# Moving the preparation of head pairs, the first loads and the norm steps within the schedule of a routed-attention and SwiGLU kernel

## The chip, the cores and the metric

The kernel runs on one core of a Trainium2 chip. The metric is the time of one execution in device microseconds, lower is better.

## The reference, cut to what matters

```python
# q, k, v: (4, 8, 768, 64); centroids: (8, 16, 64)
q_assign = argmax(q_n @ c_n, axis=-1)            # 16 clusters
k_assign = argmax(k_n @ c_n, axis=-1)
mask = q_assign[..., :, None] == k_assign[..., None, :]
attn = softmax(where(mask, q @ k.T / 8, -1e9))
x = attn @ v                                     # then per token:
xn = x / rms(x) * rms_g                          # (3072, 512)
out = (silu(xn @ w_gate) * (xn @ w_val)) @ w_out # d_ff 1536
```

## The kernel before

The program is one loop over 288 steps, nine per head, in which the instructions of all engines are written in an order set by hand. A pair of heads therefore takes 18 steps, and there are 16 pairs. A step writes a piece of the scores of the current head and their exponential, from step 96 on a piece of the feed-forward network of an earlier batch, one group of PV matmuls of the previous head, and whatever has been put on that step.

```python
def t_group(g):                      # transposes q or k of one head on PE
    ...
    on_dve = (g % 2 == 0 if pi == 0 else g > 1 if pi == 1 else pi < 6 or g % 2)
    if on_dve: nc.vector.tensor_copy(dst, tp)     # out of PSUM
    else:      nc.scalar.copy(dst, tp)
# casts(), casts_v(): POOL.  assign(): PE, scores against the centroids (sp)
# argmax1(): DVE, tr and mx.  argmax2(): DVE, oh, oh, ohT
# place(): DMA of the one-hot rows into the tiles that the scores read
return [t_group(0..3), casts, assign, argmax1, argmax2, place, casts_v]
...
def pv_norm(slot):                   # attention's own division
    nc.vector.reciprocal(inv, acc[:, :, D:D + 1])
    nc.vector.tensor_tensor(x, acc[:, :, 0:D], inv, op=ALU.mult)
...
def ffn_piece(n, kind, ...):         # kind 0: gp, 1: vp, 2: dp
    # PSUM tiles of gp and vp: two buffers in turn
    # DVE frees gp with uu, and vp with gvT; both are put on the list pend
...
for step in range(NT):
    slot, j = divmod(step, NCH)      # NCH = 9
    score_chunk(slot, j)
    ffn_next(...)
    flush(1)                         # writes out pend but for its last entry
    if slot > 0 and 2 <= j < 2 + ST: pv_group(slot - 1, j - 2)   # j = 2..7
    if slot > 0 and j == 2 + ST:     pv_norm(slot - 1)           # j = 8
    extras(step)                     # preparation, norms, loads
```

Up to step 95 the scores go in chunks of three steps through one wide exponential, and all transposes share one PSUM tile. "RMS norm" below is the second normalization (`ir`, `xn`), which comes after attention.

The softmax here doesn't subtract the row's maximum and nothing guards it: scores larger than these inputs give would overflow.

Of the kernel before, what the change touches and what calls it, by code (L numbers as in the profile page):

```python
# [19 lines left out]
def kernel(  # L20
# [12 lines left out]
    nc = tc.nc  # L33
    B, H, S, D = q.shape
# [10 lines left out]
    NCH = ST * S // CH  # L45
# [33 lines left out]
    def load_part(pi, kind):  # L79
        b, hp = divmod(pi, NP)  # L80
        src, nm = ((q, "q_in"), (k, "k_in"), (v, "v_in"))[kind]
        src = src[b, 2 * hp:2 * hp + 2]
        tl = ld.tile([P, 2, ST * D], F32, name=nm, tag=nm)
        nc.sync.dma_start(out=tl, in_=src.rearrange("h (p t) d -> p h (t d)", p=P))
        loads.setdefault(pi, []).append(tl)

    def load_pair(pi):
        for kind in range(3):
            load_part(pi, kind)

    c_in = const.tile([P, D], F32, name="c_in")
    nc.scalar.dma_start(out=c_in, in_=centroids.rearrange("h c d -> (h c) d"))
    for pi, kinds in ((0, (0, 1)), (1, (0, 1)), (0, (2,)), (1, (2,)), (2, (0, 1, 2))):
        for kind in kinds:
            load_part(pi, kind)
    g_b = const.tile([P, DM], F32, name="g_b")
# [25 lines left out]
    def keep_warm(n):  # L122
        w_ps = ps_first.tile([P, CH], F32, name="w_ps", tag="f")
        for _ in range(n):
            nc.tensor.matmul(w_ps, lhsT=zeros[:, 0:P], rhs=zeros, start=True, stop=True)
# [31 lines left out]
    def w_load(i):  # L157
        if i < 8:
            j, kind = divmod(i, 2)
            c = slice(j * DF // 4, (j + 1) * DF // 4)  # L160
            nc.gpsimd.dma_start(out=(wg, wv)[kind][:, :, c],
                                in_=(moe_w_gate, moe_w_val)[kind][:, c].rearrange("(c p) f -> p c f", p=P))
        else:
            j = i - 8
            nc.gpsimd.dma_start(
                out=wo[:, 3 * j:3 * j + 3, :],
                in_=moe_w_out[j * 3 * P:(j + 1) * 3 * P, :].rearrange("(c p) d -> p c d", p=P))
# [4 lines left out]
    def t_tile(name):  # L172
        nt[0] += 1
        pool, tag = ps_t, "t"
        if "wide" not in late:
            pool, tag = ps_first, "f"
        elif "t" in late and nt[0] % 2:
            pool = late["t"]
        return pool.tile([P, HS], F32, name=name, tag=tag)

    def prep_parts(pi):
        st = pi % NSET
        qk32 = [None]
        state = {}

        def t_group(g):
            a, side = divmod(g, 2)
            if g == 0:
                qk32[0] = prep.tile([P, 4, HS], F32, name="qk32", tag="qk32")
            tp = t_tile("tp")  # L190
            src = loads[pi][side]
            for i in range(TH):
                nc.tensor.transpose(tp[:, i * P:(i + 1) * P], src[:, a, i * P:(i + 1) * P], ident_f)  # L193
            dst = qk32[0][:, g, :]
            on_dve = (g % 2 == 0 if pi == 0 else g > 1 if pi == 1 else pi < 6 or g % 2)
            if on_dve:
                nc.vector.tensor_copy(dst, tp)  # L197
            else:
                nc.scalar.copy(dst, tp)  # L199
            state[g] = tp  # L200

        def casts():
            if pi == 0:
                for g in range(4):
                    a, side = divmod(g, 2)
                    for par in range(2):
                        dst = aug[0][a][0:D, side, par * HS:(par + 1) * HS]
                        src = state[g][par * D:(par + 1) * D, :]
                        if g == 3:
                            nc.vector.tensor_copy(dst, src)  # L210
                        else:
                            nc.scalar.copy(dst, src)
                return
            for a in range(2):
                for par in range(2):
                    nc.gpsimd.tensor_copy(aug[st][a][0:D, :, par * HS:(par + 1) * HS],  # L216
                                          qk32[0][par * D:(par + 1) * D, 2 * a:2 * a + 2, :])

        def casts_v():
            v_in = loads[pi][2]  # L220
            nc.gpsimd.tensor_copy(vbf[st][:, :, :, 0:D],  # L221
                                  v_in[:, :, :].rearrange("p a (t d) -> p a t d", d=D))

        def assign():
            h0 = 2 * (pi % NP)
            sp = t_tile("sp")
            for j in range(4):
                side, a = divmod(j, 2)
                nc.tensor.matmul(sp[32 * j:32 * j + 32, :], lhsT=cbd[:, h0 + a, :, :].rearrange("p c r -> p (c r)"),  # L229
                                 rhs=qk32[0][:, 2 * a + side, :], start=True, stop=True,  # L230
                                 tile_position=(0, 32 * j))
            state["sp"] = sp

        def argmax1():
            tr = prep.tile([P, HS], F32, name="tr", tag="tr")
            nc.vector.transpose(tr, state["sp"])  # L236
            mx = small.tile([P, TH * 4, 2], F32, name="mx", tag="mx")
            trv = tr[:, :].rearrange("p (n c r) -> p n r c", c=NC, r=2)
            nc.vector.tensor_reduce(mx, trv, axis=AX, op=ALU.max)
            state["tr"], state["mx"] = trv, mx  # L240

        def argmax2():
            oh = prep.tile([P, HS], BF16, name="oh", tag="oh")
            nc.vector.tensor_tensor(oh[:, :].rearrange("p (n c r) -> p n r c", c=NC, r=2), state["tr"],  # L244
                                    state["mx"].unsqueeze(3).to_broadcast([P, TH * 4, 2, NC]), op=ALU.is_ge)
            nc.vector.tensor_scalar(oh[0:64, :], oh[0:64, :], scalar1=1.0, scalar2=MASK,
                                    op0=ALU.subtract, op1=ALU.mult)
            ohT = prep.tile([P, HS], BF16, name="ohT", tag="ohT")
            nc.vector.transpose(ohT, oh)
            state["ohT"] = ohT  # L250

        def place():
            ohT = state["ohT"]
            for a in range(2):
                for side in range(2):
                    r = 32 * (2 * side + a)
                    eng = nc.sync
                    if pi == 0:
                        eng = nc.gpsimd if side else nc.scalar
                    eng.dma_start(out=aug[st][a][D:KA, side, :].rearrange("c (r n) -> c r n", r=2),  # L260
                                  in_=ohT[r:r + 2 * NC, :])

        return [lambda: t_group(0), lambda: t_group(1), lambda: t_group(2), lambda: t_group(3), casts, assign, argmax1, argmax2, place, casts_v]


# [167 lines left out]
    def at(step, fn):  # L433
        extra.setdefault(step, []).append(fn)

    T0, T1, T2, T3, CAST, SP, ARG1, ARG2, PLACE, CASTV = range(10)
    p0, p1 = prep_parts(0), prep_parts(1)
# [9 lines left out]
    p1[T0]()  # L447
    p0[ARG2]()
    p0[PLACE]()
    for i in (T1, T2, T3, CAST):  # L450
        p1[i]()
    keep_warm(8)
    for i in (SP, ARG1, ARG2, PLACE, CASTV):
        p1[i]()
    first.close()
    late["wide"] = wide.enter_context(tc.tile_pool(name="ps_wide", bufs=2, space=PSUM))
    load_pair(3)
    at(4, lambda: load_pair(4))
    at(30, lambda: nc.sync.dma_start(out=g_b, in_=moe_rms_g.unsqueeze(0).to_broadcast([P, DM])))
    for pi in range(2, B * NP):  # L460
        base = 2 * NCH * (pi - 2) + {2: 4, 3: 1, 6: 6}.get(pi, 0)
        steps = (0, 2, 4, 6, 7, 9, 10, 12, 12, 10) if pi < 7 else (0, 1, 3, 4, 5, 8, 9, 11, 11, 9)
        for fn, step in zip(prep_parts(pi), steps):
            at(base + step, fn)
        if pi < B * NP - 3:
            at({6: 100, 7: 106}.get(pi, base + 12), lambda pi=pi: load_pair(pi + 3))
    for i, step in enumerate((50, 58, 68, 76, 86, 94, 100, 105, 111, 117, 123, 129)):
        at(step, lambda i=i: w_load(i))
    for b in range(B):
        steps = (9, 9, 10, 10, 11, 12, 13, 15, 17, 19, 20, 22, 24, 26)  # L470
        for fn, step in zip(rms_parts(b), steps):
            at(H * NCH * (b + 1) + step, fn)

    def extras(step):
        for fn in extra.get(step, ()):
            fn()
# [1 line left out]
    for step in range(NT):  # L478
        slot, j = divmod(step, NCH)
# [10 lines left out]
            pv_norm(slot - 1)  # L490
        extras(step)

    for j in range(28):
        if j < LAG:
            ffn_next(2 * FC * (B - 1))
        else:
            ffn_next(NU, tail=True)
        flush(1)
        if 2 <= j < 2 + ST:
            pv_group(NS - 1, j - 2)  # L500
        if j == 2 + ST:
            pv_norm(NS - 1)
        extras(NT + j)
# [32 lines left out]
```

## Time and profile before

The kernel before takes 366.14 us (median of four runs, 365.24 to 367.71; the prediction counts from one of them, 366.76). What matters of the profile, whose span is 364.7 us:

| stage | us | what limits it |
|---|---|---|
| to step 95 | 0 to 79 | PE and ACT in turn, many short waits, half clock for 10.24 us |
| steps 96 to 287 | 79 to 285 | PE, nearly without gaps |
| tail of the feed-forward | 285 to 365 | PE |

### The profile page before, as it was taken

What the parts mean: (1) busy time and instruction counts of PE and PEld (TensorE: products, weight loads), DVE (VectorE), ACT (ScalarE), POOL (GpSimd) and SP (SyncE); (2) the same over time, 40 slices, a digit from 0 to 9 for tenths busy, and PEclk for the clock granted to TensorE, in tenths of its full rate; (3) what the DMA queues carried; (4) which work ended last, traced back from release to release, by engine and by line L of the source; (5) the groups of instructions that cost most, each with busy time, mean ns of one, the idle gap of its engine ahead of it and who ended that gap; (6) DMA issues with size and microseconds to landing.
All of it is one profiled execution on the core that took longest, in us unless ns stands there. A gap on an engine that the chain in (4) does not pass through costs nothing.

```text
span 364.7 us, 7453 instructions
## 1 busy us (share of the span) xinstructions
PE 340.2 (93%) x2930; PEld 204.5 (56%) x2930; DVE 222.0 (61%) x443; ACT 228.0 (63%) x395; POOL 85.8 (24%) x119
## 2 busy tenths in 40 slices
PE   7878997688999999999999999999999979999996
PEld 4446665355666665656565665656666635555542
DVE  4766663667666648695665658695544586555540
ACT  3487888656787776867676767767777343232321
POOL 2554551762414041321204041320000011000000
PEclk9999999679999999999999999999999999999999
DMA  7449499289992310735051001431000013100012
GB/s 242 160 136 291 158 217 209 62 112 113 281 221 103 113 58 25 192 75 168 0 164 38 12 31 36 49 78 38 29 2 31 30 51 86 38 31 29 31 58 86
DMA packets 38242, 35.38 MB, mean 97 GB/s; under 512 B 15072, under 2 KB 35008, under 8 KB 38208
## 3 DMA queue, kind: packets, MB, share of 16 engines
q1 hardware_dynamic: 32080, 30.06, 27.8%
q0 software_dynamic: 5888, 4.77, 9.4%
q8 instruction: 23, 0.38, 0.4%
q10 hardware_dynamic: 240, 0.08, 0.1%
q14 instruction: 11, 0.09, 0.1%
HBM read 28.61 MB, written 6.29 MB: 96 GB/s over the span
## 4 chain that ended last, share of the span: by engine, by line
PE 75%; DVE 13%; ACT 5%; DMA 3%; issue 2%; POOL 1%; ACTq 0%; DVEq 0%
PE dp L401 15%; PE vp L372 15%; PE gp L372 15%; PE sc L287 9%; PE acc L301 7%; PE tp L193 6%; PE scw L287 4%; DVE xn L343 3%; PE sp L229 3%; DMA q_in<-in_q_dram 3%; ACT pT L290 2%; DVE gvT L387 1%; ACT jk L326 1%; DVE oh L244 1%; DVE qk L197 1%
## 5 line engine op out<-in xcount | busy, mean ns | idle before, releaser
L290 ACT ACTIVATE pT<-sc 128x512 bf16<-128x512 f32 x192 | 113.3, 597 | 54.7 <-PE sc L287 53.6
L381 DVE SCALAR_TENSOR_TENSOR uu<-th,gp 128x384 f32<-128x384 f32 x96 | 53.0, 553 | 72.9 <-ACT th L377 72.6
L372 PE MATMUL vp<-xnT,wv 128*128 128x384 bf16 x384 | 78.1, 325 | 2.6 <-DVE gvT L387 2.3
L372 PE MATMUL gp<-xnT,wg 128*128 128x384 bf16 x384 | 78.1, 325 | 1.2 <-DVE uu L381 1.0
L401 PE MATMUL dp<-wo,gvT 128*128 128x512 bf16 x288 | 76.0, 378 | 2.9 <-ACT ob L407 1.5
L377 ACT ACTIVATE th<-gp 128x384 f32<-128x384 f32 x96 | 47.1, 491 | 47.9 <-PE gp L372 44.9
L216 POOL CAST aug<-qk 64x768 bf16<-64x768 f32 x60 | 52.1, 868 | 103.8 <-DVE qk L197 100.6
L301 PEld LDWEIGHTS <-pT 128*128 128x128 bf16 x1152 | 58.5, 98 | 29.1 <-issue 3.4
L287 PE MATMUL sc<-aug 80*128 80x512 bf16 (+1 forms) x256 | 72.9, 326 | 0.0
L301 PE MATMUL acc<-vbf,pT 128*128 128x65 bf16 x1152 | 64.3, 195 | 0.2 <-DVE x L311 0.2
L387 DVE TENSOR_TENSOR gvT<-uu,vp 128x384 bf16<-128x384 f32 x96 | 52.6, 548 | 6.5 <-PE vp L372 1.4
L372 PEld LDWEIGHTS <-wg 128*128 128x128 bf16 x384 | 37.2, 97 | 30.2 <-issue 2.3
L290 ACT ACTIVATE pT<-scw 128x1536 bf16<-128x1536 f32 x32 | 45.0, 1452 | 14.4 <-PE scw L287 14.2
L372 PEld LDWEIGHTS <-wv 128*128 128x128 bf16 x384 | 37.0, 97 | 22.3 <-issue 4.2
L401 PEld LDWEIGHTS <-gvT 128*128 128x128 bf16 x288 | 27.9, 97 | 29.1 <-issue 4.4
L287 PEld LDWEIGHTS <-aug 80*128 80x128 bf16 x384 | 34.0, 98 | 17.7 <-POOL vbf L221 4.4
L197 DVE COPY qk<-tp 128x384 f32<-128x384 f32 x40 | 22.1, 554 | 25.6 <-PE tp L193 25.6
L287 PE MATMUL scw<-aug 80*128 80x512 bf16 (+1 forms) x128 | 27.2, 337 | 1.9 <-DVE tr L236 0.7
L334 POOL TENSOR_SCALAR ir<-ss 128x3 f32<-128x3 f32 x8 | 1.6, 196 | 97.8 <-ACT jk L326 97.8
L343 DVE SCALAR_TENSOR_TENSOR xn<-x,ir,g_b 128x512 bf16<-128x512 bf16 x24 | 20.5, 863 | 5.5 <-POOL ir L335 5.4
L193 PE MATMUL tp<-ident_f,k_in 128*128 128x128 f32 x96 | 17.7, 296 | 5.3 <-ACT qk L199 4.3
L193 PE MATMUL tp<-ident_f,q_in 128*128 128x128 f32 x96 | 17.8, 298 | 3.0 <-DMA q_in<-in_q_dram 2.0
(54 smaller groups left out, 204.2 us busy)
## 6 DMA issues: line engine op xcount, KB each, us to landing
q_in<-in_q_dram SPq DMA_DIRECT2D x16, 384.0 KB, 4.7
k_in<-in_k_dram SPq DMA_DIRECT2D x16, 384.0 KB, 5.1
v_in<-in_v_dram SPq DMA_DIRECT2D x16, 384.0 KB, 5.7
out_dram<-ob SPq DMA_DIRECT2D x24, 256.0 KB, 2.0
wg<-in_moe_w_gate_dram POOLq DMA_DIRECT2D x4, 384.0 KB, 5.4
wv<-in_moe_w_val_dram POOLq DMA_DIRECT2D x4, 384.0 KB, 6.7
wo<-in_moe_w_out_dram POOLq DMA_DIRECT2D x4, 384.0 KB, 7.2
aug<-ohT SPq DMA_DIRECT2D x60, 24.0 KB, 1.9
```

The lines of the kernel that those rows point to most:

```text
L193: nc.tensor.transpose(tp[:, i * P:(i + 1) * P], src[:, a, i * P:(i + 1) * P], ident_f)
L197: nc.vector.tensor_copy(dst, tp)
L216: nc.gpsimd.tensor_copy(aug[st][a][0:D, :, par * HS:(par + 1) * HS], qk32[0][par * D:(par + 1) * D, 2 * a:2 * a + 2, :])
L287: nc.tensor.matmul(sc[:, o:o + n], lhsT=ag[:, 1, kc * P:(kc + 1) * P], rhs=ag[:, 0, qo:qo + n], start=True, stop=True)
L290: nc.scalar.activation(pts[slot][:, j * CH:(j + nch) * CH], sc[:, :nch * CH], ACT.Exp, scale=scale)
L301: nc.tensor.matmul(acc[:, TORD[g], :], lhsT=pts[slot][:, kc * S + g * P:kc * S + (g + 1) * P], rhs=vb[:, a, TORD[kc], :], start=(kc == 0), ...
L343: nc.vector.scalar_tensor_tensor(st["xn"][:, tl, :], x_t[b][:, t, :], st["ir"][:, tl:tl + 1], g_b, op0=ALU.mult, op1=ALU.mult)
L372: nc.tensor.matmul(pt[:, :HS], lhsT=w[:, dc, fc * P:(fc + 1) * P], rhs=xnT[b, m][:, :, dc, :], start=(dc == 0), stop=(dc == DC - 1))
L377: nc.scalar.activation(th, pt[:, :HS], ACT.Tanh, scale=0.5)
L381: nc.vector.scalar_tensor_tensor(uu, th, 1.0, pt[:, :HS], op0=ALU.add, op1=ALU.mult)
L387: nc.vector.tensor_tensor(gvT[half][:, fc, :], uu, pt[:, :HS], op=ALU.mult)
L401: nc.tensor.matmul(dp, lhsT=gvT[hf][:, f, tl * P:(tl + 1) * P], rhs=wo[:, f, :], start=(f == 0), stop=(f == FC - 1))
```

## The change

The intent was to let the first one-hot DMAs pass ahead of the third pair's loads, to start scores before the second pair is assigned, and to prepare each pair earlier, so that preparation and RMS norm do not meet.

```diff
-    for pi, kinds in (..., (1, (2,)), (2, (0, 1, 2))):
+    for pi, kinds in (..., (1, (2,))):
-            on_dve = (... g > 1 if pi == 1 else pi < 6 or g % 2)
+            on_dve = (... g > 0 if pi == 1 else pi < 7 or g % 2)
-                    if pi == 0:
-                        eng = nc.gpsimd if side else nc.scalar
+                    if pi == 0 and side:
+                        eng = nc.gpsimd
...
     p0[PLACE]()
+    load_pair(2)
...
-    for i in (SP, ARG1, ARG2, PLACE, CASTV):
-        p1[i]()
-    load_pair(3)
-    at(4, lambda: load_pair(4))
+    for i, step in ((SP, 0), (ARG1, 0), (ARG2, 1), (PLACE, 1), (CASTV, 1)):
+        at(step, p1[i])
+    at(2, lambda: load_pair(3))
+    at(6, lambda: load_pair(4))
...
-        base = 2 * NCH * (pi - 2) + {2: 4, 3: 1, 6: 6}.get(pi, 0)
-        steps = (0, 2, 4, 6, 7, 9, 10, 12, 12, 10) if pi < 7 else (0, 1, 3, 4, 5, 8, 9, 11, 11, 9)
+        base = 2 * NCH * (pi - 2) + {2: 7, 3: 2}.get(pi, 0)
+        steps = (-3, -1, 1, 3, 4, 6, 7, 8, 8, 10) if pi < 8 else (-3, -2, 0, 1, 2, 5, 6, 7, 7, 10)
...   (the RMS norm, now written ahead of the preparation of the same step)
-        steps = (9, 9, 10, 10, 11, 12, 13, 15, 17, 19, 20, 22, 24, 26)
+        steps = (9, 9, 10, 11, 12, 13, 15, 18, 20, 22, 23, 25, 28, 31)
-    for j in range(28):
+    for j in range(33):
```

The entries of `steps` for preparation are, in order: four transposes, casts, assignment, argmax1, argmax2, place, cast of v.

More of the change, by code (lines that the diff above doesn't have):

```diff
@@ L92 @@
     nc.scalar.dma_start(out=c_in, in_=centroids.rearrange("h c d -> (h c) d"))
-    for pi, kinds in ((0, (0, 1)), (1, (0, 1)), (0, (2,)), (1, (2,)), (2, (0, 1, 2))):
+    for pi, kinds in ((0, (0, 1)), (1, (0, 1)), (0, (2,)), (1, (2,))):
         for kind in kinds:
@@ L194, in t_group @@
             dst = qk32[0][:, g, :]
-            on_dve = (g % 2 == 0 if pi == 0 else g > 1 if pi == 1 else pi < 6 or g % 2)
+            on_dve = (g % 2 == 0 if pi == 0 else g > 0 if pi == 1 else pi < 7 or g % 2)
             if on_dve:
@@ L452 @@
     keep_warm(8)
-    for i in (SP, ARG1, ARG2, PLACE, CASTV):
-        p1[i]()
     first.close()
     late["wide"] = wide.enter_context(tc.tile_pool(name="ps_wide", bufs=2, space=PSUM))
-    load_pair(3)
-    at(4, lambda: load_pair(4))
+    for i, step in ((SP, 0), (ARG1, 0), (ARG2, 1), (PLACE, 1), (CASTV, 1)):
+        at(step, p1[i])
+    at(2, lambda: load_pair(3))
+    at(6, lambda: load_pair(4))
     at(30, lambda: nc.sync.dma_start(out=g_b, in_=moe_rms_g.unsqueeze(0).to_broadcast([P, DM])))
+    for b in range(B):
+        steps = (9, 9, 10, 11, 12, 13, 15, 18, 20, 22, 23, 25, 28, 31)
+        for fn, step in zip(rms_parts(b), steps):
+            at(H * NCH * (b + 1) + step, fn)
     for pi in range(2, B * NP):
-        base = 2 * NCH * (pi - 2) + {2: 4, 3: 1, 6: 6}.get(pi, 0)
-        steps = (0, 2, 4, 6, 7, 9, 10, 12, 12, 10) if pi < 7 else (0, 1, 3, 4, 5, 8, 9, 11, 11, 9)
+        base = 2 * NCH * (pi - 2) + {2: 7, 3: 2}.get(pi, 0)
+        steps = (-3, -1, 1, 3, 4, 6, 7, 8, 8, 10) if pi < 8 else (-3, -2, 0, 1, 2, 5, 6, 7, 7, 10)
         for fn, step in zip(prep_parts(pi), steps):
@@ L468 @@
         at(step, lambda i=i: w_load(i))
-    for b in range(B):
-        steps = (9, 9, 10, 10, 11, 12, 13, 15, 17, 19, 20, 22, 24, 26)
-        for fn, step in zip(rms_parts(b), steps):
-            at(H * NCH * (b + 1) + step, fn)
     def extras(step):
```

## The prediction

> **What bounds the kernel now.** I read the busy shares first, then a table by stage, then the order of time where a stage is not full.
>
> ```profile
> PE 340.2 (93%) x2930; PEld 204.5 (56%) x2930; DVE 222.0 (61%) x443; ACT 228.0 (63%) x395; POOL 85.8 (24%) x119
> ...
> PEclk9999999679999999999999999999999999999999
> ```
>
> ```profile
> 0.00:80.00 80.00, 65.82 (x660) 41.36 (x661) 47.53 (x100) 55.91 (x58) 38.98 (x59) 0.94 0.70 181
> 80.00:100.00 20.00, 18.64 (x185) 11.55 (x183) 14.37 (x29) 14.49 (x29) 8.92 (x12) 1.00 0.93 175
> 100.00:280.00 180.00, 177.93 (x1612) 109.45 (x1611) 115.84 (x233) 129.75 (x251) 35.86 (x46) 1.00 0.28 75
> 280.00:340.00 60.00, 57.44 (x376) 32.04 (x375) 36.48 (x69) 22.08 (x48) 2.09 (x4) 1.00 0.15 44
> ```
>
> Columns of the table: stretch, its length, then busy time of PE, PEld, DVE, ACT and POOL, the granted clock, DMA share and GB/s. From 100 to 280 us PE is idle 180 - 177.93 = 2.1 us in all. The change does not alter PE's work, so this stage can give only those 2.1 us; 280 to 340 holds 2.6 us and 80 to 100 holds 1.4 us. The large gap is the first 80 us: 80 - 65.82 = 14.2 us idle, and a clock below full in two slices of 9.1 us. In finer windows the clock is 0.5 from about 67 to 77.3 us.
>
> In this stage scores leave PSUM in chunks of 128x1536, through one exponential each: 32 of 1.40 us (45.0 us over 32). ACT's timeline starts the group of three at 34.81, 44.28 and 53.75, so a pair of heads (18 steps, six chunks) takes 9.47 us when all goes well, of which 6 x 1.40 = 8.4 is ACT's exponentials. The last six chunks, steps 78 to 95, do not: the first starts at 53.75 + 4 x 6.82/5 = 59.2, and the narrow scores of step 96 start at 78.6. That is 19.4 us against 9.47. The timeline there:
>
> ```profile
> 60.41 0.53 ACT L199 COPY qk<-tp 128x384 f32<-128x384 f32 x1
> ...
> 60.99 0.55 PE L193 MATMUL tp<-ident_f,k_in 128*128 128x128 f32 x3 [1.52 <-ACT qk L199]
> ...
> 64.77 0.55 PE L193 MATMUL tp<-ident_f,k_in 128*128 128x128 f32 x3 [0.95 <-ACT qk L199]
> ...
> 66.64 1.30 DVE L343 SCALAR_TENSOR_TENSOR xn<-x,ir,g_b 128x512 bf16<-128x512 bf16 x1 [3.82 <-POOL ir L335]
> 67.86 0.54 DVE L197 COPY qk<-tp 128x384 f32<-128x384 f32 x1
> ...
> 68.45 1.50 PE L229 MATMUL sp<-qk,cbd 128*32 128x384 f32 x8 [1.93 <-DVE qk L197]
> ...
> 71.72 1.45 ACT L290 ACTIVATE pT<-scw 128x1536 bf16<-128x1536 f32 x1 [3.09 <-PE scw L287]
> ```
>
> Columns: start, length, engine and line, tiles, and in brackets the idle time and what ended it. Pair 6 is transposed here through the one PSUM tile of this stage; half its copies stand on ACT behind an exponential, so PE waits 1.52 and 0.95. Then the norm of the first batch (xn) sits in DVE's order, waits 3.82 for its factors, and blocks the last copy of pair 6, for which PE waits 1.93. The clock halves just then, and ACT starves for 3.09.
>
> [...] half clock lasts 10.24 us, [...] and the four matmuls of a chunk go from 0.81 to 1.47 us. [...] SP issuing pair 3's q_in only at 21.89 after four one-hot DMAs. [...] the one-hot compare took 0.93 us under POOL's casts at 16.87, and 0.59 otherwise.
>
> **The change, part by part.** No operation is removed; everything is order and engine.
>
> *Head.* Before:
>
> ```profile
> 15.52 0.10 PEld L287 LDWEIGHTS <-aug 80*128 80x128 bf16 x1 [0.62 <-DMA aug<-ohT]
> 15.67 0.58 DVE L236 STREAM_TRANSPOSE tr<-sp 128x384 f32<-128x384 f32 x1 [1.93 <-PE sp L229]
> ...
> 16.30 1.46 PE L287 MATMUL scw<-aug 80*128 80x512 bf16 x8 [0.71 <-DVE tr L236]
> ...
> 19.67 0.55 PE L193 MATMUL tp<-ident_f,k_in 128*128 128x128 f32 x3 [0.16 <-DVE qk L197]
> ```
>
> The first scores need the one-hot DMAs (there at 15.52) and a PSUM pool freed when pair 1's argmax has read its scores (16.25). With pair 1's assignment moved below the first chunk only the DMA remains: first scores at 15.5, 0.8 earlier. Holding back pair 2 frees little: its loads were over by 13 us in the packet record, before the one-hot DMAs start moving at 14. But pair 1's argmax now starts at about 17.1 (chunk 0.65, sp 0.85) rather than 15.67. Its five DVE operations take 2.6 to 3.2 us, after which comes pair 2's first copy, which ends at about 20.4 rather than 19.6. PE's next transposes and chunk 3 slip by some 0.8. Pair 2's loads, issued from about 14.1, land near 18 (the first load of all took 3.87) and hardly matter. Pair 1's one-hot DMAs come 0.8 later, so pair 3's q_in too, issued near 22.7 and landing near 27 to 28.5 (5.83 before). PE already waited 1.29 us for it at step 19; now the transpose stands at step 17, ahead of the chunk of step 18. I take +1.2 us in all by step 20: the early start is more than given back.
>
> *Pairs 3 to 5.* Preparation three steps sooner has many steps of slack and does not shorten a chain. Transposes now alternate with chunk and PV work; PE's waits for DVE copies, 1.9 us in five waits between 16 and 58, may shrink: -0.4.
>
> *Pair 6.* Moved from steps 78-90 to 69-82, and its copies all on DVE. Steps 67-78 ran at 6.82/5 = 1.36 us a chunk with no preparation; at the regular 9.47/6 = 1.58, three chunks cost 0.22 x 3 = +0.7. Steps 78-96 then hold only pair 7 and the norm of batch 0. ACT there: exponentials 8.4, four sums of squares of 0.62 + 0.19 = 3.3, two copies of 0.48 = 1.0, together 12.7. Add the regular loss of 9.47 - 8.4 = 1.1, and 1.2 for pair 7's copies, which still alternate (k transposes and the next chunk, 0.5 + 0.65, stand behind an ACT copy): 15.0 against 19.4, so -4.4. This assumes full clock. In the changed order no copy on which PE waits stands behind xn in DVE, so the 1.93 goes and with it the likely trigger.
>
> *Norms.* The factors get one more step before the first xn in each batch, and later parts are spread out; pair preparation from pair 8 on ends its argmax before the norm. The 80-100 stage keeps 0.5 of 1.4 idle: -0.9. The waits at 141 and 223 us (0.7 of PE each, behind an output copy behind xn): -1.2 together. In the tail PE waits 0.42, 1.05 and 0.32 between 296 and 299 for the same reason: -0.8. Five more loop turns in the tail only make room for later norm steps.
>
> Sum: 1.2 - 0.4 + 0.7 - 4.4 - 0.9 - 1.2 - 0.8 = -5.8, so 361.0 us from 366.76.
>
> **The rivals.** *The head opens a new clock drop.* PE could sit two microseconds at 26-28 waiting for q_in of pair 3, with chunk 6 behind it. For it: [...] the slip above. Against it: before had 1.29 us there without a drop. [...] *The drop at 67 comes again.* Pair 7's copies on ACT still hold PE for about 2 us, as the 1.52 and 0.95 above; [...] half of the 4.4 is lost: 363 to 364. Against: no xn block beside it. *The early stage is bound by ACT and the work just moves:* DVE copies of pair 6 stretch steps 69-78 by more than 0.7 and the end stands still: 366. *All waits behind xn go entirely:* up to 2.5 us more from the main stage and tail, and pair 6's stretch near 13 us: 357.
>
> **Range and chances.** I give the two clock rivals together about one in four, with 3 to 4 us each, so about +0.9: 361.9, rounded to 361.8. Low end: everything hidden, 356.5. High end: clock drop and head loss, 367. Faster by over 2% means below 359.4, which needs 1.6 us more than my sum: 0.22. Slower by over 2% needs 374, for which nothing in the profile speaks: 0.02.
>
> **What would show it.** First scores near 15.5 us; pair 3's first transpose waiting for q_in near 28 and chunk 7's exponential 1 to 2 us later than 29.25; steps 78-96 in about 15 us, with no half clock; PE idle in 100-280 near 1 us; xn's wait for ir under 1 us or harmless. I am wrong if the clock still halves, if the head gains rather than loses, or if the stage after 100 us, full in PE, gets longer.

No term of the sum is cut: 1.2 - 0.4 + 0.7 - 4.4 - 0.9 - 1.2 - 0.8 = -5.8, so 361.0 us from 366.76. The +0.9, for two clock rivals of 3 to 4 us each, stands as an estimate of mine. From the trace alone, the one stretch of 10.24 us at a clock of 0.5 costs, by estimate, at most 10.24 / 2 = 5.1 us. The prediction stays 361.8 us, range 356.5 to 367.

## The result, and the profile after

The changed kernel takes 383.3 us (median of four runs, 381.6 to 384.81): 4.6% slower, ratio 1.0463 (95% interval 1.0402 to 1.0523). A ratio here is the mean time of one kernel's fast runs over that of the other's of the same rounds, so not quite the ratio of the medians. The predicted range ended at 367. All outputs are right.

The page of the changed kernel, busy shares and the clock slice by slice:

```profile
PE 345.8 (91%) x2930; PEld 208.1 (55%) x2930; DVE 223.2 (59%) x446; ACT 228.3 (60%) x392; POOL 85.6 (23%) x119
...
PEclk9898999978999999999999999998999999999999
```

No engine has more work, apart from PE's 5.6 us more of busy time; this goes with more matmuls at half clock (the four of a chunk took 0.81 us at 65.53 in the kernel before and 1.47 at 70.21, where the clock was 0.5). The clock is half in five stretches of 20.5 us together, where it was one of 10.24 (a last drop as the work ends, in both, is left out). The same table of stretches as in the prediction (stretch, length, busy time of PE, PEld, DVE, ACT, POOL, clock, DMA share, GB/s):

```profile
0.00:80.00 80.00, 66.07 (x648) 41.55 (x649) 44.91 (x101) 54.27 (x53) 35.76 (x56) 0.92 0.68 176
80.00:100.00 20.00, 16.88 (x139) 10.40 (x138) 11.94 (x24) 11.67 (x24) 7.87 (x11) 0.88 0.92 184
100.00:280.00 180.00, 169.67 (x1536) 104.72 (x1534) 114.61 (x223) 122.95 (x238) 39.88 (x50) 0.99 0.28 74
```

The first 80 us look like before. The stage that was full is not: from 100 to 280 us PE is idle 180 - 169.67 = 10.3 us, where it was 2.1. To place the loss by work rather than by time, I compared when the exponential of the same step starts in the two traces:

| step | before, us | after, us | lag, us |
|---|---|---|---|
| 0 | 17.20 | 16.39 | -0.8 |
| 18 | 26.93 | 29.67 | 2.7 |
| 36 | 37.49 | 41.74 | 4.3 |
| 78 | 59.08 | 65.93 | 6.9 |
| 96 | 79.06 | 80.12 | 1.1 |
| 108 | 91.31 | 96.73 | 5.4 |
| 144 | 126.69 | 135.08 | 8.4 |
| 240 | 236.84 | 249.67 | 12.8 |
| 252 | 249.89 | 265.19 | 15.3 |
| 282 | 279.47 | 294.76 | 15.3 |

The lag grows in the head, grows again pair by pair, falls by 5.8 between steps 78 and 96, and then grows with every pair until the last pair is prepared (its last part stands at step 244). After that it stands still. The start itself is uncertain by some 2 us: with an unchanged head, the profiled runs have step 0 anywhere from 15.65 to 17.20 us. What counts is how the lag grows.

**What PE waits for in the full stage.** The view of waits from 100 to 280 us (who waits for whom: us in total, times, longest), first before, then after:

```profile
PE vp L372 <- DVE gvT L387: 0.5, 1, 0.5
```

```profile
PE vp L372 <- DVE gvT L387: 10.3, 9, 1.8
```

One wait of PE accounts for the idle time: a vp matmul may not start because DVE has not freed its PSUM buffer. The timeline of one such place after:

```profile
122.49 0.56 DVE L381 SCALAR_TENSOR_TENSOR uu<-th,gp 128x384 f32<-128x384 f32 x1 [0.29 <-ACT th L377]
...
122.96 0.58 DVE L244 TENSOR_TENSOR oh<-tr,mx 128x384 bf16<-128x384 f32 x1
...
123.30 0.90 POOL L221 CAST vbf<-v_in 128x768 bf16<-128x768 f32 x1 [2.88 <-issue]
...
123.58 0.73 DVE L246 TENSOR_SCALAR oh<-oh 64x384 bf16<-64x384 bf16 x1
...
124.34 0.58 DVE L249 STREAM_TRANSPOSE ohT<-oh 128x384 bf16<-128x384 bf16 x1
...
125.04 0.56 DVE L311 TENSOR_TENSOR x<-acc,inv 128x384 bf16<-128x384 f32 x1
125.51 0.54 DVE L387 TENSOR_TENSOR gvT<-uu,vp 128x384 bf16<-128x384 f32 x1
...
126.11 0.81 PE L372 MATMUL vp<-xnT,wv 128*128 128x384 bf16 x4 [0.98 <-DVE gvT L387]
```

And the corresponding lines of before:

```profile
116.02 0.56 DVE L311 TENSOR_TENSOR x<-acc,inv 128x384 bf16<-128x384 f32 x1
116.50 0.54 DVE L387 TENSOR_TENSOR gvT<-uu,vp 128x384 bf16<-128x384 f32 x1
...
119.41 0.58 DVE L244 TENSOR_TENSOR oh<-tr,mx 128x384 bf16<-128x384 f32 x1
...
120.82 0.52 DVE L387 TENSOR_TENSOR gvT<-uu,vp 128x384 bf16<-128x384 f32 x1
```

Read the order of DVE. Before, attention's division (inv, x) and the one-hot part of the argmax (oh, oh, ohT) stand in different gaps between feed-forward operations: at steps 8 and 11. After, they stand at steps 8 and 7, between uu and the gvT that PE waits for. Because step 8 writes a dp piece, which leaves nothing to flush, that gvT is not written before step 9, so it comes after both. From the start of uu to the start of gvT DVE needs 125.51 - 122.49 = 3.0 us, and in those steps (j = 8, 0, 1) PE has no PV groups with which to fill the time. Two things add up here: the neighbours, and what I call a collision, an overlap with work on POOL in which the DVE operation takes longer. POOL's cast of v starts at 123.30, just as PV of step 7 ends (its last matmuls start at 122.82 and take 0.34), and the second oh, 0.62 us of it beside the cast, takes 0.73 in place of 0.25.

**The wide stage.** For pairs 4 to 7 argmax1 now stands ahead of attention's division (steps 7 and 8 of the pair). After:

```profile
46.25 0.55 DVE L239 TENSOR_REDUCE mx<-tr 128x24 f32<-128x384 f32 x1
...
46.94 0.56 DVE L311 TENSOR_TENSOR x<-acc,inv 128x384 bf16<-128x384 f32 x1
...
47.64 0.34 PE L301 MATMUL acc<-vbf,pT 128*128 128x65 bf16 x6 [1.14 <-DVE x L311]
```

Before, in the pair that corresponds, the division came first:

```profile
42.42 0.56 DVE L311 TENSOR_TENSOR x<-acc,inv 128x384 bf16<-128x384 f32 x1
...
43.37 0.58 DVE L236 STREAM_TRANSPOSE tr<-sp 128x384 f32<-128x384 f32 x1 [0.40 <-PE sp L229]
```

The single accumulator of PV comes free late, PE waits 1.14 us, and so does the next chunk behind it. ACT's groups of three start at 52.40 and 63.04, a period of 10.64 us per pair in place of 9.47.

**Pair 7 and the RMS norm.** Between steps 96 and 108 the lag grows by 4.3; e4, which puts pair 7's argmax back, does not have this growth (below). The timeline:

```profile
82.47 0.88 POOL L335 TENSOR_TENSOR ir<-ir,mhalf 128x3 f32<-128x3 f32 x1
...
87.22 0.52 DVE L387 TENSOR_TENSOR gvT<-uu,vp 128x384 bf16<-128x384 f32 x1
...
87.79 1.10 PE L372 MATMUL vp<-xnT,wv 128*128 128x384 bf16 x4 [2.95 <-DVE gvT L387]
```

Here xn, tr, mx, the division, oh, oh and ohT all stand ahead of one gvT, the xn late (0.91 us of waiting) because its factors stand on POOL behind two casts (79.71, 1.71 us) and a DMA issue (81.37, 0.75 us). PE waits 2.95 us, and at 88.18 the clock halves.

**The head.** The first scores came when predicted, at 15.48 us, though this proves little, as starts vary:

```profile
15.48 0.82 PE L287 MATMUL scw<-aug 80*128 80x512 bf16 x4 [1.99 <-DMA aug<-ohT]
...
28.41 0.52 PE L193 MATMUL tp<-ident_f,q_in 128*128 128x128 f32 x3 [1.27 <-DMA q_in<-in_q_dram]
```

But pair 1's assignment used to occupy PE while it waited for the one-hot DMAs. Now PE is idle for 1.99 us there, and the clock halves at 16.5 us.

### The profile page after: what moved, and what is told of

The parts are those of the page before. It is cut to its first block, busy times and chain, and to the rows that moved or that the text cites. A ratio compares the mean times of both kernels' runs of the same rounds, so it can differ in the third digit from the quotient of the medians.

```text
span 379.7 us, 7464 instructions
## 1 busy us (share of the span) xinstructions
PE 345.8 (91%) x2930; PEld 208.1 (55%) x2930; DVE 223.2 (59%) x446; ACT 228.3 (60%) x392; POOL 85.6 (23%) x119
## 3 DMA queue, kind: packets, MB, share of 16 engines
q1 hardware_dynamic: 32176, 30.11, 26.5%
## 4 chain that ended last, share of the span: by engine, by line
PE 75%; DVE 16%; ACT 3%; issue 2%; POOL 2%; DMA 2%; DVEq 0%; ACTq 0%; POOLq 0%
PE dp L401 15%; PE vp L372 15%; PE gp L372 14%; PE sc L287 9%; PE acc L301 8%; PE tp L193 6%; PE scw L287 4%; PE sp L229 3%; DVE oh L244 2%; DVE x L311 2%; DVE ohT L249 2%; DVE oh L246 2%; DVE gvT L387 2%; DVE qk L197 1%; DVE xn L343 1%
## 5 line engine op out<-in xcount | busy, mean ns | idle before, releaser
L372 PE MATMUL vp<-xnT,wv 128*128 128x384 bf16 x384 | 78.9, 328 | 14.1 <-DVE gvT L387 14.0
L372 PE MATMUL gp<-xnT,wg 128*128 128x384 bf16 x384 | 79.4, 329 | 0.4 <-DVE uu L381 0.4
L301 PEld LDWEIGHTS <-pT 128*128 128x128 bf16 x1152 | 60.3, 100 | 32.8 <-issue 9.2
L216 POOL CAST aug<-qk 64x768 bf16<-64x768 f32 x60 | 50.4, 841 | 117.3 <-DVE qk L197 72.0
L287 PE MATMUL sc<-aug 80*128 80x512 bf16 (+1 forms) x256 | 73.8, 331 | 0.0
L301 PE MATMUL acc<-vbf,pT 128*128 128x65 bf16 x1152 | 66.0, 197 | 3.4 <-POOL vbf L221 2.3
L287 PEld LDWEIGHTS <-aug 80*128 80x128 bf16 x384 | 34.4, 100 | 20.5 <-issue 8.4
L197 DVE COPY qk<-tp 128x384 f32<-128x384 f32 x43 | 23.7, 555 | 28.6 <-PE tp L193 28.6
L287 PE MATMUL scw<-aug 80*128 80x512 bf16 (+1 forms) x128 | 28.7, 350 | 2.2 <-DMA aug<-ohT 2.0
L221 POOL CAST vbf<-v_in 128x768 bf16<-128x768 f32 x16 | 14.8, 924 | 34.9 <-issue 24.6
L343 DVE SCALAR_TENSOR_TENSOR xn<-x,ir,g_b 128x512 bf16<-128x512 bf16 x24 | 17.7, 747 | 4.1 <-POOL ir L335 4.1
```

Of the source, the lines that this page charges most:

```text
L216: nc.gpsimd.tensor_copy(aug[st][a][0:D, :, par * HS:(par + 1) * HS], qk32[0][par * D:(par + 1) * D, 2 * a:2 * a + 2, :])
L287: nc.tensor.matmul(sc[:, o:o + n], lhsT=ag[:, 1, kc * P:(kc + 1) * P], rhs=ag[:, 0, qo:qo + n], start=True, stop=True)
L301: nc.tensor.matmul(acc[:, TORD[g], :], lhsT=pts[slot][:, kc * S + g * P:kc * S + (g + 1) * P], rhs=vb[:, a, TORD[kc], :], start=(kc == 0), ...
L343: nc.vector.scalar_tensor_tensor(st["xn"][:, tl, :], x_t[b][:, t, :], st["ir"][:, tl:tl + 1], g_b, op0=ALU.mult, op1=ALU.mult)
L372: nc.tensor.matmul(pt[:, :HS], lhsT=w[:, dc, fc * P:(fc + 1) * P], rhs=xnT[b, m][:, :, dc, :], start=(dc == 0), stop=(dc == DC - 1))
```

## The experiments

Twelve kernels ran in three groups. Each diff is against the kernel named first. Times are medians of four runs (six for e8); the kernel before had medians of 367.2 to 367.3 in these groups. The changed kernel was not run again in them, so a comparison with it is a difference of two ratios to the kernel before, each with its own interval: about 3 us either way. By the medians such differences come out 0.3 to 0.9 us smaller than the figures given below.

**e1_head**: before, with the head of the change alone.

```diff
(the loads of pair 2, on_dve of pair 1, the DMA engine, pair 1's
 steps 0 and 1, the loads of pairs 3 and 4, as in the change)
```

> The kernel before with only the head of the change (third pair's loads held back behind the first one-hot DMAs, those DMAs on SP, second pair's assignment beneath the first scores, loads of pairs 3 and 4 two steps later). Theory (the head loses what the exponentials' start times show in the changed kernel, +2.75 us by step 18 and more where the clock halves near 30 us): 2.5 to 4.5 us slower than before, first exponential about 0.8 us earlier, step 18 about 2.7 us later. Rival (the head's lag is absorbed, the whole loss lies in the later table of steps): within 1 us of before.

Measured: 369.51 us, ratio 1.0073 (1.0031 to 1.0115). The theory holds: the head loses 2.7 us, and in the trace the lag stays near 2.1 from step 18 to step 90 rather than being absorbed. In that trace the clock is half from 15.55 us on for 10.24 us.

**e2_prep**: before, with the new preparation steps alone.

```diff
(base and steps of the preparation, and pi < 7 in on_dve, as in the change)
```

> The kernel before with only the new table of preparation steps (and pair 6's copies on DVE). Theory (DVE's order: the argmax of a pair now stands directly around the norm of the attention output, so that the release of PSUM for PE's next matmuls comes late, once per pair): 8 to 12 us slower than before, PE waits for gvT of about 1 us per pair in the stage from 100 to 280 us, a period of about 10.6 us per pair before it. Rival (the loss comes from the head and its clock drops, or from the new norm steps together with the early preparation): less than 4 us slower.

Measured: 380.29 us, ratio 1.0361 (1.0284 to 1.0437), that is 13 us, more than the 8 to 12 expected. PE's waits for gvT between 100 and 280 us are 11.7 us in 11 waits. The table of preparation steps is the cause of most of the loss, with the old head and the old RMS norm beside it. In the profiled run the head too had a half clock (18.46 us, 10.24 long) and step 18 came 3.7 us late, with the head unchanged, so the size is no pure measure of the table. But two of the four runs were granted a mean clock of 0.995, above every run of the kernel before beside them (0.971 to 0.981), and still took 377.98 and 378.31 us: some 11 us of this loss are not half clock.

**e3_norms**: before, with the new RMS norm steps alone.

```diff
(steps of rms_parts, their place ahead of the preparation, range(33))
```

> The kernel before with only the new table of norm steps (spread out, put before the preparation within a step, five more turns in the tail). Theory: small gain, 0 to 2 us faster than before, since the waits of PE behind xn at 141, 223 and 296 us go. Rival (the wait of DVE for the factors on POOL behind casts and a DMA issue, seen at 79 to 84 us of the changed kernel, comes from the new norm steps): 2 to 5 us slower.

Measured: 365.48 us, ratio 0.9969 (0.991 to 1.0027). The best estimate is a gain of 1.1 us; the interval reaches from 3.3 us faster to 1.0 slower. The rival (2 to 5 us slower) falls: the norm steps alone do no such harm. In the trace, from 100 to 280 us, PE's waits of 1.4 us for DVE's output copy (dp for ob) are gone, but those for gvT rise from 0.5 to 1.4.

**e4_argmax_back**: the changed kernel, argmax of pairs 4, 5 and from 7 on put back.

```diff
+        if pi in (4, 5, 7):
+            steps = (-3, -1, 1, 3, 4, 9, 10, 12, 12, 10)
+        elif pi > 7:
+            steps = (-3, -2, 0, 1, 2, 8, 9, 11, 11, 9)
```

> The changed kernel with only the assignment, argmax and one-hot DMA of pairs 4, 5 and from 7 on put back to the steps they had (3 to 4 steps later within the pair), transposes and casts still three steps early. Theory (argmax next to the norm in DVE's order is the cause): about 11 to 15 us of the 17 come back, 368 to 372 us, the waits of PE for gvT in the stage 100 to 280 us fall from 10 us to under 2. Rival (early transposes and POOL casts, or clock drops of their own, are the cause): 378 us or more, waits as in the changed kernel.

Measured: 364.91 us, ratio 0.9922 (0.987 to 0.9974). More comes back than I expected: all of it, although transposes and casts are still three steps early and the head is still the new one. PE's waits for gvT are 1.6 us. So the early transposes cost nothing that shows; what costs is the place of the argmax in these pairs, with the collision that comes with it (e12). For pairs from 8 on the cast of v also went back here, from step 10 to 9; e11 keeps it at 10, and so rules it out as the cause.

**e5_late_adjacent**: before, argmax moved later, so that it becomes the neighbour of the division of the pair's second head.

```diff
+        if pi > 7:
+            steps = (0, 1, 3, 4, 5, 14, 15, 16, 16, 9)
```

> The kernel before with nothing of the change but the adjacency: from pair 8 on, the preparation keeps its old, late transposes, and its assignment, argmax and one-hot DMA move later, to steps 14, 15 and 16, directly ahead of the norm of the pair's second head at step 17 (the changed kernel has 5, 6 and 7 ahead of the norm at step 8). Theory (it is the neighbours in DVE's order that cost, not being early): 6 to 9 us slower than before, 372 to 376 us, waits of PE for gvT of about 10 us between 100 and 280 us. Rival (early transposes or casts cost): within 2 us of before, waits under 2 us.

Measured: 369.65 us, ratio 1.0098 (1.0033 to 1.0163). Late adjacency costs as well, so being early is not the cause; but it costs 3.6 us and not 6 to 9, with 3.8 us of waits for gvT. The size was a miss. Two differences of this place show in the traces. The cast of v does not collide: oh and oh take 0.58 and 0.25 for all eight pairs, while in the changed kernel each of the eight pairs has either a second oh of 0.73 or a compare of 1.21. And the next pair's first transposes are written at step 18, so PE has work while DVE catches up. The first of these is tested in e12; the second was not tested by itself.

**e6_hold_only**: before, loads of pair 2 held back and the query side of the one-hot DMAs on SP.

```diff
-    ..., (1, (2,)), (2, (0, 1, 2))):
+    ..., (1, (2,))):
-                    if pi == 0:
-                        eng = nc.gpsimd if side else nc.scalar
+                    if pi == 0 and side:
+                        eng = nc.gpsimd
     p0[PLACE]()
+    load_pair(2)
```

> The kernel before with only the third pair's loads held back behind the first one-hot DMAs and the query side of those DMAs on SP. Theory (the loads were over before the one-hot DMAs moved, so holding back wins nothing, and pair 2 and 3 are delayed a little): 0 to 2 us slower, first exponential not earlier by more than 0.3 us. Rival (the load traffic delays the one-hot DMAs): first exponential earlier by 0.5 us or more and a faster kernel.

Measured: 367.02 us, ratio 0.9995 (0.9947 to 1.0044). It changes nothing in the time. Its profiled run started its first exponential at 15.12, not 17.20, though, which is the sign I had given to the rival. The start is no clean sign: e5, whose head is unchanged, started at 15.65. So the time alone decides, and by it nothing is won.

**e7_assign_only**: before, pair 1's assignment beneath the first scores.

```diff
-    for i in (SP, ARG1, ARG2, PLACE, CASTV):
-        p1[i]()
+    for i, step in ((SP, 0), (ARG1, 0), (ARG2, 1), (PLACE, 1), (CASTV, 1)):
+        at(step, p1[i])
(with pair 1's copies and the loads of pairs 3 and 4 as in the change)
```

> The kernel before with only the second pair's assignment beneath the first scores (and the loads of pairs 3 and 4 at steps 2 and 6, the copies of pair 1 split as in the change). Theory: first exponential 0.8 us or more earlier, but step 18 about 1 to 2 us later, since pair 3's loads on SP wait behind pair 1's later one-hot DMAs; 1 to 3 us slower. Rival (the early scores are kept, the hold-back alone costs): 0 to 1 us faster than before.

Measured: 370.54 us, ratio 1.009 (1.0038 to 1.0143), a loss of 3.3 us, a little over the 1 to 3 expected. Within the noise this is the head's whole loss. Its trace has PE idle for 2.59 us before the first scores, half clock from 16.85 us for 10.24 us, and step 18 at 30.11 us, 3.2 late where 1 to 2 were expected. The seven profiled kernels with this part of the change (the changed one, e1, e4, e7, e9, e11, e12) all have a half clock that begins between 14 and 22 us; of the seven without it two have (e2 and e3).

**e8_best**: a version meant to beat both.

```diff
(before, with the RMS norm steps of the change and pi < 7 in on_dve)
-        base = ... {2: 4, 3: 1, 6: 6}.get(pi, 0)
+        base = ... {2: 4, 3: 1}.get(pi, 0)
-        steps = (0, 2, 4, 6, 7, 9, 10, 12, 12, 10) if pi < 7 else (0, 1, 3, 4, 5, 8, 9, 11, 11, 9)
+        steps = (0, 2, 4, 6, 7, 9, 10, 12, 12, 10) if pi < 8 else (-3, -2, 0, 1, 2, 8, 9, 11, 11, 9)
+        if pi in (4, 5, 7):
+            steps = (-3, -1, 1, 3, 4, 9, 10, 12, 12, 10)
+        elif pi == 6:
+            steps = (-3, -1, 1, 3, 4, 6, 7, 8, 8, 10)
```

> A version meant to beat both: head of before, norm steps of the change, preparation three steps early from pair 4 on, with the argmax of all but pair 6 at the old distance from the norm, pair 6 as in the change. Theory: 1 to 2 us of the gain of e4_argmax_back, plus the 2 to 3 us that the head costs: 361 to 363.5 us. [...]

Measured: 360.75 us (359.38 to 361.62), ratio 0.9821 (0.9785 to 0.9856), just below the expected band: faster than both. The gain is clear of noise; whether it is over 2% is not. Its page:

```profile
PE 336.2 (94%) x2930; PEld 202.4 (56%) x2930; DVE 219.5 (61%) x445; ACT 227.0 (63%) x393; POOL 85.1 (24%) x119
...
PEclk9999999999999999999999999999999999999999
```

PE is busy 4 us less than before for the same 2930 matmuls, and no slice has a low clock.

**e9_main_back**: the changed kernel, argmax of pairs 8 to 15 alone put back.

```diff
+        if pi > 7:
+            steps = (-3, -2, 0, 1, 2, 8, 9, 11, 11, 9)
```

> The changed kernel with the argmax put back to its old distance (steps 8, 9, 11) for pairs 8 to 15 alone. Theory (the loss of the stage from 100 us on is argmax next to the norm, once per pair): 9 to 11 us faster than the changed kernel, 372 to 375 us; the lag of the exponentials against before no longer grows between steps 108 and 240. Rival (the lag there is carried by pair 7 and the norms): 380 us or more.

Measured: 371.7 us, ratio 1.0123 (1.007 to 1.0176), a little below the expected band. These eight pairs carry 1.0463 - 1.0123 = 3.4% of the time, about 12.5 us. What e4 puts back besides, pairs 4, 5 and 7, carries 1.0123 - 0.9922 = 2.0%, about 7.4 us. The two traces divide this: e9's exponentials are 0.2 us ahead of e4's at step 36, 2.4 behind at step 78, 1.8 at step 96 and 6.1 at step 108. So pairs 4 and 5 cost some 2.5 us, and pair 7, whose argmax stands at steps 96 to 98, some 4.3 (one profile each).

**e10_pair6_only**: before, with nothing but pair 6 earlier and on DVE.

```diff
+        if pi == 6:
+            base, steps = 2 * NCH * (pi - 2), (-3, -1, 1, 3, 4, 6, 7, 8, 8, 10)
(and pi < 7 in on_dve)
```

> The kernel before with nothing but pair 6 prepared nine steps sooner and its copies all on DVE. Theory (this is the part of the change that pays: 5.8 us between steps 78 and 96 in the changed kernel, and no half clock at 67 us): 3.5 to 6 us faster than before, 361 to 363.5 us. Rival (the gain of the best version came from the early transposes of all pairs): within 2 us of before.

Measured: 363.23 us, ratio 0.9899 (0.9853 to 0.9946), a gain of 3.7 us. In the profiled run the half clock did not vanish, it fell from 10.24 to 6.83 us, so that part of the expectation was a miss.

**e11_main_earlier**: the changed kernel, argmax of pairs 8 to 15 earlier still.

```diff
+        if pi > 7:
+            steps = (-3, -2, 0, 1, 2, 4, 5, 6, 6, 10)
```

> The changed kernel with assignment, argmax and one-hot DMA of pairs 8 to 15 one step earlier still (4, 5, 6 in place of 5, 6, 7), so that they no longer stand between uu of step 6 and the norm of step 8 in DVE's order. Theory (neighbours in the order, not earliness): 5 to 9 us faster than the changed kernel, 374 to 378 us. Rival (the earlier, the worse): 383 us or more.

Measured: 371.54 us, ratio 1.0132 (1.008 to 1.0185): about 12 us come back by moving three parts one step further in the direction that had been thought harmful. That is more than the 5 to 9 expected, and the clearest test that being early is not the cause. It takes away the neighbours and the collision at once (the second oh takes 0.25 in all eight pairs), so it does not tell the two apart. The timeline of DVE at such a place:

```profile
121.70 0.58 DVE L249 STREAM_TRANSPOSE ohT<-oh 128x384 bf16<-128x384 bf16 x1
122.21 0.52 DVE L381 SCALAR_TENSOR_TENSOR uu<-th,gp 128x384 f32<-128x384 f32 x1
...
123.34 0.54 DVE L387 TENSOR_TENSOR gvT<-uu,vp 128x384 bf16<-128x384 f32 x1
```

The one-hot part is over before uu, and gvT starts 1.1 us after it, not 3.0.

**e12_vcast_act**: the changed kernel, cast of v of pairs 8 to 15 on ACT.

```diff
-            nc.gpsimd.tensor_copy(vbf[st][:, :, :, 0:D], v_in...)
+            cast = nc.scalar.copy if pi > 7 else nc.gpsimd.tensor_copy
+            cast(vbf[st][:, :, :, 0:D], v_in...)
```

> The changed kernel with the cast of v of pairs 8 to 15 on ACT in place of POOL. In the changed kernel POOL's cast starts as the last PV matmuls end, just when DVE runs the one-hot step, and that step takes 0.73 or the compare 1.21 us in place of 0.25 and 0.58. Theory (about half of the loss per pair is this collision of POOL and DVE): 3 to 6 us faster than the changed kernel, 377 to 380 us, the one-hot step back at 0.25. Rival (only the order counts): within 1.5 us of the changed kernel.

Measured: 376.27 us, ratio 1.025 (1.02 to 1.0299), about 7.8 us better than the changed kernel. The second oh, in DVE's timeline at the place of the changed kernel's 0.73:

```profile
124.12 0.25 DVE L247 TENSOR_SCALAR oh<-oh 64x384 bf16<-64x384 bf16 x1
```

PE's waits for gvT fall from 10.3 to 6.2 us. The gain is above the expected 3 to 6; by the start of the exponentials, 2.3 us of the profiled lead come between steps 240 and 252, where the changed kernel had a half clock at 255 us and this one none. Between steps 108 and 252, the stage of these pairs, the lag grows by 9.9 us in the changed kernel, 4.1 here and 3.4 in e5 (order without collision), and by nothing in e9 and e11 (-1.1 and -0.2). So the loss of these pairs has two parts: the order alone accounts for less than half, and the rest goes with the collision. A collision without this order was not run.

## Why the prediction was wrong

*Bound of the kernel, and where it could gain.* Right. The first 80 us and the stretch at 67 us were the places with something to win.

*Pair 6.* Right that it pays, and in size, but by luck in part. The prediction's 0.7 - 4.4 = -3.7 us was measured by itself in e10 as -3.7, and in the changed kernel steps 78 to 96 take 14.2 us (80.12 - 65.93), where 15.0 were predicted. But the 15.0 assumed full clock, and "the clock still halves" was a sign of being wrong: it halved at 74.52 for 6.83 us, and in e10 at 69.94 for 6.83. The trigger that I had named was the wait behind xn; in the kernel before, the clock fell 0.54 us into that wait of 1.93. What came true is the second clock rival, pair 7's copy on ACT:

```profile
73.81 0.55 PE L193 MATMUL tp<-ident_f,k_in 128*128 128x128 f32 x3 [1.95 <-ACT qk L199]
```

In e10 the same wait is 2.31. Without a half clock (e8) the steps take 13.4 us, so the 15.0 was 1.6 too long, and the half clock hid that.

*Pairs 3 to 5.* Here the prediction failed: "Preparation three steps sooner has many steps of slack and does not shorten a chain." I looked at who uses the result of a preparation, and how late it may come, and not at who stands behind it in DVE's order. The -0.4 us were +7.4 for pairs 4, 5 and 7 together, by the difference of e9 and e4, of which the traces give some 2.5 to pairs 4 and 5, each with one PE wait of 1.14 us at that place. Pair 3, whose argmax still follows the division, was not put back by itself. Pair 7's some 4.3 answer another term: the stage from 80 to 100 us was to keep 0.5 us of PE idle time and has 20 - 16.88 = 3.1, nearly all of it the one wait of 2.95 behind pair 7's argmax, the division and xn.

*Pairs 8 to 15.* The larger failure is in half a sentence: "pair preparation from pair 8 on ends its argmax before the norm". I meant the RMS norm, and counted it as a gain. The other normalization, attention's division at steps 8 and 17 of every pair, was not looked at. The argmax now ended just ahead of that one, and the term that was not in the sum at all is about 12.5 us (e9; 11.6 by the medians). The prediction named the sign to look for, a longer stage after 100 us, but gave it no weight; the chance of 0.02 for a slower kernel was far too small for a change that touches a full stage in every pair.

*Head.* The direction was right: the early start is given back. +1.2 us were +2.7 (e1) to +3.3 (e7). The transpose of pair 3 did wait for q_in at 28.41, and chunk 7 was 2.8 us later. What was mis-sized is the term for PE's idle time before the one-hot DMAs, which I had counted as nothing: it goes with a half clock in every profiled kernel that has it. I had looked for the rival clock drop at 26 to 28 us; the changed kernel has one at 30.15 too, but the one at 16.5 was not foreseen.

*RMS norm.* -0.9 - 1.2 - 0.8 = -2.9 us were about -1.1 in e3, whose interval (-3.3 to +1.0) holds both -2.9 and zero: neither the step nor its size is settled by the time.

*The sum.* With the ratios as shares of 367 us: e9's part 3.4%, pairs 4, 5 and 7 2.0%, head 0.7%, pair 6 -1.0%, RMS norm -0.3%, together 4.8%, against 4.6% measured for the whole. The first two are differences from the changed kernel itself, so they add up by construction; what is tested is that head, pair 6 and RMS norm, measured alone (-0.6% together), agree with e4, which has all three (-0.8%). No large interaction shows.

*What stays open.* How much of each part is the wait and how much the half clock that follows it was not separated, except that e2's two runs at a clock of 0.995 leave some 11 us to other causes than the clock. A kernel that only keeps the clock up was not built. Nor was the effect of PE's spare work at the place of e5 measured by itself.

## What to carry to other kernels

In a schedule written by hand, an operation moved earlier has a cost even when its result is not urgent: ask what now stands behind it in the order of its engine, and whether a PSUM buffer is freed there. In a stage where PE is full, look at the longest run of operations of the freeing engine between two releases, and spread it; here one step earlier was enough (e11), and so was three to four steps later (e9). Split a change that moves several tables at once: here one part of it was worth 3.7 us and the rest hid it.

## What the traces show of the clock, and of DVE beside POOL

- In the 3.41 us before a drop of the clock, the longest idle time of PE was 0.95 us in the kernel before (67.07 us), and 1.99, 1.27, 1.95, 2.95 and 1.79 us at the five drops of the changed one. In these two traces all changes of the clock lie on one grid of 3.41 us (half clock lasts 10.24 us in the first; 3.41, 3.41, 6.83, 3.41 and 3.41 in the second), and PE's idle time within one stretch of that grid goes with a drop, though not alone. Of the stretches from 8 to 350 us that began at full clock, the three with 1.95 us or more idle all ended in a drop, and none with 1.29 us or less did; of the six between, those with 1.79, 1.49 and 1.48 did, and those with 1.80, 1.77 and 1.64 did not.
- The collisions have these sizes: in the changed kernel, beside a cast of v on POOL of 0.90 to 1.22 us (0.82 to 0.83 in the kernel before), a 64x384 bf16 operation with two scalars went from 0.25 to 0.73 us and a compare of two inputs from 0.58 to 1.21; in the kernel before, the compare took 0.80 to 0.93 at the four places where it overlapped a cast. Taking that cast off POOL (e12) went with 7 to 8 us of 383.
